# Halved feed-forward steps moved side by side into a block's first half, with their VectorE chains alternating

## The chip, the cores and the metric

The kernel runs on one NeuronCore of one Trainium2 chip. The metric is the device time of one execution in microseconds (us). The kernel before takes 614.94 us, the median of 3 runs (614.88 to 615.11). Engine names are those of the profile: PE is TensorE, DVE VectorE, ACT ScalarE, POOL GpSimd, SP SyncE. An engine's queue runs strictly in the order in which the kernel's Python emits its instructions.

## The reference

`x` is 8 x 3008 x 256 in f32. The first stage is the real part of a two-dimensional Fourier transform over the sequence (3008) and the features (256); the second is a feed-forward layer over the 24,064 tokens:

```python
X = np.fft.fft(np.fft.fft(x, axis=1), axis=2).real      # 8 x 3008 x 256
h = np.maximum(X.reshape(24064, 256) @ w_in, 0.0)       # w_in 256 x 2048
out = (h * h) @ w_out                                   # w_out 2048 x 256
```

## The kernel before

**What is computed.** The transform over the features is multiplied into `w_in` (the three tables `gh`), so that the kernel has only the transform over the sequence left, in f16: `zc` (cosine half) and `zs` (sine half), 128 feature rows by token columns. Symmetry makes one column serve two tokens, k and S-k: with p = gh0·zc and q = gh1·zs, the two tokens' hidden values are p + q and p - q, apart from a term for the row d = 128, which sits in row 0 of `zs`.

**Blocks and steps.** The 12,040 columns are cut into 25 windows (240, 512, 376, 376, 512, 448, eighteen of 512, 360), one block each, numbered from 0. A block has 8 steps; a step makes 256 of the 2048 hidden rows, for both tokens of the window's columns. During block w the second feed-forward product of block w-1 runs as well (`ffn2_steps`, L618, 16 matmuls of 256 columns a step), and so does the Fourier product of the image half whose columns begin in block w+1 (`z_steps`, L480: 12 matmuls of 376 columns for a half called e = 0, 20 shorter ones for e = 1; none in some blocks). Each Fourier half gives `zc` and `zs`: a first sum goes to `es` (ACT, L485); after the second sum ACT writes the near columns (L489) and DVE the far ones ("minus", L496).

**A plain step** (`pq`, `turn`, `square`): four matmuls of p + q (L730, L731), ACT takes max(.,0) into a buffer `h1` (L740), DVE squares `h1` into `h2` (L745) or, for the steps in `by_act`, ACT does (L743); two more matmuls turn the sum into p - q (L736), and ACT and DVE do the same again. `h1` has three buffers, the hidden values' PSUM tile `ph` two.

**A halved step** (`half_q`, `half_p`) saves two matmuls: q alone (L755), ACT writes -2q to `sn` (L758), p is added (L764), ACT copies p + q to `hd` (L767), and DVE makes the rest: two rows `eb`·`wv` for the d = 128 term (L769), their sum with `sn` (L770), the second token's values (L771), max (L773) and square (L774) of both. The first three are called the row sum here, the last three the halves. `sn` has two buffers, `hd` four.

**The d = 128 row** (`row_spread`): ACT's queue sends row 0 of the next block's `zs` to DRAM (`zr`, L579), and SP's queue reads it back into all 128 partitions (`eb`, L581). SP's queue also issues all stores of the output (L598), behind the output's PSUM evacuations by ACT (L633).

**What sets the order.** The order is written out by hand. `PLAN` gives the halved steps and the `by_act` steps of each block by a load number: `load` counts 2 if the block has the second part of an image's folding (`fold_at`), 1 if it has the first (`first_at`), 1 if it has the late folds (`late_at`). Loads of 0 and 1: blocks 3, 6, 7, 11, 14, 17 and 20 to 24, four halved steps; higher loads: 5, 8, 9, 10, 12, 13, 15, 16, 18 and 19, three; blocks 0, 1, 2 and 4 have none. The list `at[s]` holds the folding that step s emits: `d_even`, `n_cos`, `d_odd`, `n_sin`, `odds`, `even` (DVE; `d_odd` also starts the next image's load and `even` the store `scr` on POOL's queue), `back` (four reads `rb` on POOL's queue) and the late folds. `nyq` sends a few values over PE into `py` (PSUM) and back by DVE (L377). In steps 0 to 6 `others(s)` emits, in this order, `at[s]`, the 16 second-product matmuls with their evacuation, `post[s]`, and a share of the Fourier matmuls; in a plain step it stands between `square(s, 0)` and `turn(s)`, in a halved step between `half_q` and `half_p`.

Of the kernel before, what the change touches and what calls it, by code (L numbers as in the profile page):

```python
# [8 lines left out]
F32 = mybir.dt.float32  # L9
# [3 lines left out]
ALU = mybir.AluOpType  # L13

HS = 32.0
P = 128
# [3 lines left out]
def rev_dim(ap, i):  # L20

    dims = [list(d) for d in ap.ap]
    step, cnt = dims[i]
    dims[i] = [-step, cnt]
    return bass.AP(tensor=ap.tensor, offset=ap.offset + step * (cnt - 1), ap=dims)
# [3 lines left out]
def kernel(  # L29
# [14 lines left out]
    nc = tc.nc  # L44
# [12 lines left out]
    FIRST = [240, 512, 376, 376, 512, 448]  # L57
    R23 = float(2.0 ** 23)

    PLAN = {4: ((1, 2, 4, 5), (0, 3, 6)), 3: ((1, 3, 5), (2, 4, 6)), 2: ((1, 4), (0, 3, 6)), 0: ((), ())}  # L60

    RQ = (1, 3, 5, 0, 2, 4)

# [17 lines left out]
    NW = len(wins)  # L81
# [31 lines left out]
    ps_o = ctx.enter_context(tc.tile_pool(name="ps_o", bufs=2, space=bass.MemoryType.PSUM))  # L113
# [170 lines left out]
    at = const.tile([P, 2, P + 1], F32, name="at")  # L284
# [51 lines left out]
    def fold_steps(i):  # L336
# [34 lines left out]

        def nyq():

            py = ps_o.tile([P, 512], F32, name="py", tag="po")
            nc.tensor.matmul(py[:, 0:1], perm[0], od[:, 0, 0, 128:129], start=True, stop=True)
            nc.tensor.matmul(py[:, 1:6], perm[1], rev_dim(od[:, 0, 1:6, 128:129], 1).rearrange("p r o -> p (r o)"), start=True, stop=True)
            nc.vector.tensor_copy(od[:, 1, :, 0:1], py[:, 0:6].rearrange("p (r o) -> p r o", o=1))  # L377
# [148 lines left out]
    def run(*jobs):  # L526
        for j in jobs:
            j()
# [137 lines left out]
    def plan(w):  # L666

        if w < 3 or w == 4:
            return PLAN[0]
        load = 2 * (w in fold_at) + (w in first_at) + (w in late_at)  # L670
        return PLAN[(4, 4, 3)[min(load, 2)]]

    def halved(w):

        return plan(w)[0]
# [4 lines left out]
    for w in range(NW):  # L680
        g0, wn = wins[w]
        h2 = h2p.tile([P, NFC, 2 * WN], F16, name="h2", tag="h2")
        zcw, zsw = zwin(w)

        lo, hi = 0, NST - 1
        at = [[] for _ in range(NST)]
        post = [[] for _ in range(NST)]
        if w == 0:
            at[2] = [f0s["even"], f0s["back"]]
        elif w == 1:  # L690
            fj = fold_jobs(1)
            at = [[f] for f in fj[0:5]] + [[], [], []]
            post[5] = fj[5:6]
            lo, hi = 6, 7
        elif w == 2:
            te = table_steps(1)
            at = [[folds[1]["even"], lambda: te["freq"](), lambda: te["args"](0)], [lambda: te["turns"](0)], [lambda: te["mods"](0)],
                  [lambda: te["absm"](0)], [lambda: te["sins"](0)], [lambda: te["coss"](0)], [], [lambda: te["weigh"]()]]
            for st in range(4):
                at[st + 3] = at[st + 3] + f0s["late"][st : st + 1]  # L700
            at[7].append(folds[1]["back"])
        elif w in fold_at:
            fj = jobs_of.pop(fold_at[w])
            at = [fj[2:3], [], fj[3:4], fj[4:5], [], fj[6:7], fj[7:8], []]
            post[7] = fj[5:6]
        elif w == win_of(col_of[1, 1]) - 1:
            for st in range(4):
                at[st] = folds[1]["late"][st : st + 1]
            lo = 4
        if w in late_at:  # L710
            for st in range(4):
                at[st + 3] = at[st + 3] + folds[late_at[w]]["late"][st : st + 1]
        if w in first_at:
            fj = jobs_of[first_at[w]] = fold_jobs(first_at[w])
            at[0] = at[0] + fj[0:1]
            at[2] = at[2] + fj[1:2]
        if w == 2:
            at[2].append(row_weights)
        zj, zl = [], []
        for u in need[w + 1]:  # L720
            zu = z_steps(u)
            zj += [(zu, 0, 0), (zu, 1, 0), (zu, 0, 1), (zu, 1, 1)]
        f2 = ffn2_steps(*old) if old else []
        phs = {}

        def pq(s):
            ph = phs[s] = ps_h.tile([P, 2, 512], F32, name="ph", tag="psh")
            for a in range(2):
                f0 = (2 * s + a) * P
                nc.tensor.matmul(ph[:, a, 0:wn], gh[:, 0, f0 : f0 + P], zcw[:, 0:wn], start=True, stop=False)  # L730
                nc.tensor.matmul(ph[:, a, 0:wn], gh[:, 1, f0 : f0 + P], zsw[:, 0:wn], start=False, stop=True)  # L731

        def turn(s):
            for a in range(2):
                f0 = (2 * s + a) * P
                nc.tensor.matmul(phs[s][:, a, 0:wn], gh[:, 2, f0 : f0 + P], zsw[:, 0:wn], start=False, stop=True, skip_group_check=True)  # L736

        def square(s, sg):
            h1 = h1p.tile([P, 2, 512], F16, name="h1", tag="h1")
            nc.scalar.activation(h1[:, :, 0:wn], phs[s][:, :, 0:wn], AF.Relu)  # L740
            hv = rev_dim(h1[:, :, 0:wn], 2) if sg else h1[:, :, 0:wn]
            if sg == 0 and s in by_act:
                nc.scalar.activation(h2[:, 2 * s : 2 * s + 2, 0:wn], hv, AF.Square)  # L743
            else:
                nc.vector.tensor_tensor(h2[:, 2 * s : 2 * s + 2, sg * wn : (sg + 1) * wn], hv, hv, op=ALU.mult)  # L745

        two = halved(w)
        by_act = plan(w)[1]
        sns, hds = {}, {}

        def half_q(s):
            ph = phs[s] = ps_h.tile([P, 2, 512], F32, name="ph", tag="psh")
            for a in range(2):
                f0 = (2 * s + a) * P
                nc.tensor.matmul(ph[:, a, 0:wn], gh[:, 1, f0 : f0 + P], zsw[:, 0:wn], start=True, stop=True)  # L755
            i = ROT[0] % 2
            sn = sns[s] = const.tile([P, 2, 2, WN], F16, name=f"sn{i}", tag=f"w16_{i}")
            nc.scalar.activation(sn[:, 0, :, 0:wn], ph[:, :, 0:wn], AF.Copy, bias=0.0, scale=-2.0)  # L758

        def half_p(s):  # L760
            ph, sn = phs[s], sns[s]
            for a in range(2):
                f0 = (2 * s + a) * P
                nc.tensor.matmul(ph[:, a, 0:wn], gh[:, 0, f0 : f0 + P], zcw[:, 0:wn], start=False, stop=True, skip_group_check=True)  # L764
            hd = tmp.tile([P, 2, 2 * WN], F16, name="hd", tag=("tt", "tm")[ROT[0] % 2])
            ROT[0] += 1
            nc.scalar.activation(hd[:, :, 0:wn], ph[:, :, 0:wn], AF.Copy, bias=0.0, scale=1.0)  # L767
            for a in range(2):
                nc.vector.tensor_scalar(out=sn[:, 1, a, 0:wn], in0=eb[w][:, 0:wn], scalar1=wv[:, 2 * s + a : 2 * s + a + 1], scalar2=None, op0=ALU.mult)  # L769
            nc.vector.tensor_tensor(sn[:, 0, :, 0:wn], sn[:, 0, :, 0:wn], sn[:, 1, :, 0:wn], op=ALU.add)  # L770
            nc.vector.tensor_tensor(rev_dim(hd[:, :, wn : 2 * wn], 2), hd[:, :, 0:wn], sn[:, 0, :, 0:wn], op=ALU.add)  # L771
            hv = hd[:, :, 0 : 2 * wn]
            nc.vector.tensor_scalar(out=hv, in0=hv, scalar1=0.0, scalar2=None, op0=ALU.max)  # L773
            nc.vector.tensor_tensor(h2[:, 2 * s : 2 * s + 2, 0 : 2 * wn], hv, hv, op=ALU.mult)  # L774

        def others(s):
            for j in at[s]:
                j()
            for j in spread(f2, s, NST):
                j()  # L780
            for j in post[s]:
                j()
            if s == lo:
                zl[:] = [j for zu, part, h in zj for j in zu(part, h)]
            if s >= lo:
                for j in spread(zl, s - lo, hi - lo) if s < hi else []:
                    j()


        ng = 2 if w == 0 or wins[w - 1][1] < 384 < wn else 1  # L790
        for s0 in range(0, NST, ng):
            ss = range(s0, s0 + ng)
            if s0 in two:
                half_q(s0)
                others(s0)
                half_p(s0)
                continue
            for s in ss:
                pq(s)
            for s in ss:  # L800
                square(s, 0)
            if s0 == hi and w + 1 < NW and halved(w + 1):
                row_spread(w + 1)
            others(s0)
            for s in ss:
                turn(s)
            for s in ss:
                square(s, 1)
            for s in ss[1:]:
                others(s)  # L810
            if s0 < hi <= s0 + ng - 1 and w + 1 < NW and halved(w + 1):
                row_spread(w + 1)
        old = (w, h2)
# [32 lines left out]
```

## Time and profile before

| | |
|---|---|
| median of 3 runs | 614.94 us (614.88 to 615.11) |
| the profiled execution | 615.19 us, of which the span of its instructions is 612.8 us |
| PE, ACT, DVE busy | 96%, 84%, 81% of the span |
| granted PE clock | 0.999 |
| first matmul of block 7, 12, 13, 17, 18, 19, 20 | 162.70, 285.54, 308.60, 405.39, 430.17, 455.78, 480.25 us |
| last block (24) begins | 577.45 us |

A block's first matmul is its first L730 row in the trace, and a block's length is the distance to the next block's. Sums below are made against the profiled execution (612.8 us of span and 2.4 us around it); it is 0.25 us above the median of the runs.

### The profile page before, as it was taken

The numbers are of one execution on the slowest core, as the hardware profiler recorded it, in microseconds if no ns is written. First come the engines' busy times: TensorE is split into PE (matmuls) and PEld (weight loads), VectorE is DVE, ScalarE is ACT, GpSimd is POOL, SyncE is SP. The second block draws the span as 40 slices with busy tenths as digits, with TensorE's granted clock in tenths as the row PEclk, the third lists the DMA queues.
The fourth block names the chain that finished last, engine by engine and source line by source line (L and its number), as shares of the span: only waits on it lengthen the run. The fifth ranks groups of instructions, "written<-read, shape, count | busy, mean of one in ns | idle before, by whom it ended". The sixth has DMA issues, their size and how long they took to land.

```text
span 612.8 us, 11635 instructions
## 1 busy us (share of the span) xinstructions
PE 589.3 (96%) x4416; PEld 424.8 (69%) x4416; DVE 495.4 (81%) x838; ACT 517.3 (84%) x673; POOL 82.5 (13%) x125
## 2 busy tenths in 40 slices
PE   5799999999999999999999999999899999999997
PEld 2456776776677777777777777776577667677786
DVE  7887679696999898968987898858987697887880
ACT  7687788898898898998989889898789888898872
POOL 5343100012002202020023001220010200000000
PEclk9999999999999999999999999999999999999999
DMA  8927221183114623631155121551112311211112
GB/s 146 217 68 148 61 73 35 42 177 81 52 42 90 167 59 68 151 91 55 51 112 136 58 61 48 105 146 55 48 33 64 122 35 48 57 46 44 60 56 66
DMA packets 39592, 50.21 MB, mean 82 GB/s; under 512 B 4572, under 2 KB 33393, under 8 KB 39537
## 3 DMA queue, kind: packets, MB, share of 16 engines
q0 software_dynamic: 9344, 22.14, 18.0%
q1 hardware_dynamic: 29923, 27.11, 15.1%
q8 instruction: 34, 0.56, 0.4%
q10 hardware_dynamic: 270, 0.23, 0.1%
q14 instruction: 21, 0.17, 0.1%
HBM read 36.29 MB, written 27.86 MB: 105 GB/s over the span
## 4 chain that ended last, share of the span: by engine, by line
PE 61%; DVE 16%; ACT 10%; issue 5%; DMA 4%; SPq 2%; POOL 1%; DVEq 0%; ACTq 0%; POOLq 0%
PE po L618 36%; PE ph L736 5%; PE ph L730 5%; PE ph L731 5%; ACT h L740 4%; PE ph L764 3%; PE ph L755 3%; DVE h L774 3%; DMA eb<-zr 3%; DVE hd L773 2%; DVE hd L771 2%; SPq L598 2%; PE pz L480 2%; DVE h L745 2%; ACT sn L758 2%
## 5 line engine op out<-in xcount | busy, mean ns | idle before, releaser
L618 PE MATMUL po<-wout,h 128*128 128x256 f16 (+1 forms) x3024 | 362.2, 273 | 3.2 <-DVE od L377 1.1
L618 PEld LDWEIGHTS <-h 128*128 128x128 f16 (+1 forms) x3024 | 296.4, 98 | 75.3 <-DVE h L745 1.8
L740 ACT ACTIVATE h<-ph 128x1024 f16<-128x1024 f32 (+4 forms) x252 | 235.6, 962 | 28.6 <-PE ph L736 15.5
L745 DVE TENSOR_TENSOR h<-h 128x1024 f16<-128x1024 f16 (+4 forms) x189 | 118.1, 641 | 56.1 <-ACT h L740 47.9
L731 PE MATMUL ph<-zs,gh 128*128 128x512 f16 (+4 forms) x252 | 90.9, 363 | 1.2 <-DVE zs L496 0.9
L730 PE MATMUL ph<-zc,gh 128*128 128x512 f16 (+4 forms) x252 | 91.0, 363 | 1.1 <-ACT h L740 0.8
L774 DVE TENSOR_TENSOR h<-hd 128x2048 f16<-128x2048 f16 (+3 forms) x74 | 87.9, 1188 | 2.5
L767 ACT ACTIVATE hd<-ph 128x1024 f16<-128x1024 f32 (+3 forms) x74 | 73.6, 994 | 15.0 <-PE ph L764 14.6
L633 ACT ACTIVATE osb<-po 128x512 f32<-128x512 f32 (+3 forms) x95 | 54.9, 581 | 28.4 <-PE po L618 21.5
L758 ACT ACTIVATE sn<-ph 128x1024 f16<-128x1024 f32 (+3 forms) x74 | 73.4, 992 | 0.0
L736 PE MATMUL ph<-zs,gh 128*128 128x512 f16 (+4 forms) x252 | 69.9, 363 | 2.1 <-ACT h L740 1.0
L743 ACT ACTIVATE h<-h 128x1024 f16<-128x1024 f16 (+3 forms) x63 | 64.8, 1029 | 2.0
L771 DVE TENSOR_TENSOR hd<-hd,sn 128x1024 f16<-128x1024 f16 (+3 forms) x74 | 49.8, 673 | 19.4 <-ACT hd L767 13.4
L770 DVE TENSOR_TENSOR sn<-sn 128x1024 f16<-128x1024 f16 (+3 forms) x74 | 49.8, 673 | 7.4 <-ACT hd L767 0.5
L773 DVE TENSOR_SCALAR hd<-hd 128x2048 f16<-128x2048 f16 (+3 forms) x74 | 49.9, 675 | 2.5
L769 DVE TENSOR_SCALAR sn<-eb,wv 128x512 f16<-128x512 f16 (+3 forms) x148 | 44.6, 343 | 8.2 <-DMA eb<-zr 8.2
L764 PE MATMUL ph<-zc,gh 128*128 128x512 f16 (+3 forms) x148 | 42.8, 370 | 2.6 <-ACT sn L758 1.8
L731 PEld LDWEIGHTS <-gh 128*128 128x128 f16 x252 | 24.6, 98 | 27.4 <-issue 2.5
L730 PEld LDWEIGHTS <-gh 128*128 128x128 f16 x252 | 24.5, 97 | 26.5 <-issue 1.7
L755 PE MATMUL ph<-zs,gh 128*128 128x512 f16 (+3 forms) x148 | 42.9, 371 | 0.0
L423 POOL COPY xt<-xt 128x2 f16<-128x2 f16 x16 | 5.6, 379 | 215.4 <-DVE xt L406 215.4
L736 PEld LDWEIGHTS <-gh 128*128 128x128 f16 x252 | 23.2, 97 | 9.6 <-issue 4.3
(121 smaller groups left out, 377.7 us busy)
## 6 DMA issues: line engine op xcount, KB each, us to landing
out_dram<-osb SPq DMA_DIRECT2D x77, 128.0 KB
xo<-in_x_dram POOLq DMA_DIRECT2D x7, 768.0 KB
scr<-ev POOLq DMA_DIRECT2D x8, 390.0 KB, 3.9
eb<-zr SPq DMA_DIRECT2D x18, 128.0 KB
rb<-scr POOLq DMA_DIRECT2D x16, 130.0 KB
out_dram<-osb SPq DMA_DIRECT2D x12, 94.0 KB
w<-in_moe_w_in_dram POOLq DMA_DIRECT2D x2, 512.0 KB
wout<-in_moe_w_out_dram POOLq DMA_DIRECT2D x1, 1024.0 KB
```

The lines of the kernel that those rows point to most:

```text
L618: nc.tensor.matmul(po[0:m, j * D : (j + 1) * D], h2[:, fc, q : q + m], wout16[:, fc, :], start=(fc == 0), stop=(fc == NFC - 1))
L730: nc.tensor.matmul(ph[:, a, 0:wn], gh[:, 0, f0 : f0 + P], zcw[:, 0:wn], start=True, stop=False)
L731: nc.tensor.matmul(ph[:, a, 0:wn], gh[:, 1, f0 : f0 + P], zsw[:, 0:wn], start=False, stop=True)
L736: nc.tensor.matmul(phs[s][:, a, 0:wn], gh[:, 2, f0 : f0 + P], zsw[:, 0:wn], start=False, stop=True, skip_group_check=True)
L740: nc.scalar.activation(h1[:, :, 0:wn], phs[s][:, :, 0:wn], AF.Relu)
L743: nc.scalar.activation(h2[:, 2 * s : 2 * s + 2, 0:wn], hv, AF.Square)
L745: nc.vector.tensor_tensor(h2[:, 2 * s : 2 * s + 2, sg * wn : (sg + 1) * wn], hv, hv, op=ALU.mult)
L758: nc.scalar.activation(sn[:, 0, :, 0:wn], ph[:, :, 0:wn], AF.Copy, bias=0.0, scale=-2.0)
L767: nc.scalar.activation(hd[:, :, 0:wn], ph[:, :, 0:wn], AF.Copy, bias=0.0, scale=1.0)
L771: nc.vector.tensor_tensor(rev_dim(hd[:, :, wn : 2 * wn], 2), hd[:, :, 0:wn], sn[:, 0, :, 0:wn], op=ALU.add)
L773: nc.vector.tensor_scalar(out=hv, in0=hv, scalar1=0.0, scalar2=None, op0=ALU.max)
L774: nc.vector.tensor_tensor(h2[:, 2 * s : 2 * s + 2, 0 : 2 * wn], hv, hv, op=ALU.mult)
```

## The change

1. The halved steps stand side by side in a block's first half, and the `by_act` steps change: `PLAN` now has ((1, 2, 3, 4), (0, 6)) for load 0, ((1, 2, 3, 4), (0, 5, 6)) for load 1 and ((1, 2, 3), (0, 5, 6)) above. The number of halved steps of every block stays as it was.
2. A halved step's DVE work is cut in two. The row sum is emitted right behind `half_q`, ahead of `others(s)`; the halves are emitted one step later, alternating with the next step's row sum instruction by instruction, or, where the next step is plain, around its first square.
3. Of the Fourier product's second sums the sine comes first, and `row_spread` is emitted in step 6, behind `square(6, 0)` (before: in step 7, behind `square(7, 0)`).
4. `n_cos` moves from step 2 to step 5, `n_sin` from 2 to 4, `odds` from 3 to 5, `even` from 5 to 6, `back` from 6 to 7.
5. `py` takes a bank of the Fourier product's PSUM pool instead of one of the second product's (images from 2 on).

```diff
-    PLAN = {4: ((1, 2, 4, 5), (0, 3, 6)), 3: ((1, 3, 5), (2, 4, 6)), 2: ((1, 4), (0, 3, 6)), 0: ((), ())}
+    PLAN = {0: ((1, 2, 3, 4), (0, 6)), 1: ((1, 2, 3, 4), (0, 5, 6)), 2: ((1, 2, 3), (0, 5, 6))}
...
-            py = ps_o.tile([P, 512], F32, name="py", tag="po")
+            py = (ps_z if i > 1 else ps_o).tile([P, 512], F32, name="py", tag="pz" if i > 1 else "po")
...
-        load = 2 * (w in fold_at) + (w in first_at) + (w in late_at)
-        return PLAN[(4, 4, 3)[min(load, 2)]]
+        return PLAN[min(2, 2 * (w in fold_at) + (w in first_at) + (w in late_at))]
...
-            at = [fj[2:3], [], fj[3:4], fj[4:5], [], fj[6:7], fj[7:8], []]
+            at = [fj[2:3], [], [], [], fj[3:4], fj[4:5], fj[6:7], fj[7:8]]
...
-            at[2] = at[2] + fj[1:2]
+            at[5] = at[5] + fj[1:2]
...
-            zj += [(zu, 0, 0), (zu, 1, 0), (zu, 0, 1), (zu, 1, 1)]
+            zj += [(zu, 0, 0), (zu, 1, 0), (zu, 1, 1), (zu, 0, 1)]
...
+        def row_sum(s):
...
+            return [
+                lambda: row(0),
+                lambda: row(1),
+                lambda: nc.vector.tensor_tensor(sn[:, 0, :, 0:wn], sn[:, 0, :, 0:wn], sn[:, 1, :, 0:wn], op=ALU.add),
+            ]
+
+        def halves(s):
...
+            return [
+                lambda: nc.vector.tensor_tensor(rev_dim(hd[:, :, wn : 2 * wn], 2), hd[:, :, 0:wn], sn[:, 0, :, 0:wn], op=ALU.add),
+                lambda: nc.vector.tensor_scalar(out=hv, in0=hv, scalar1=0.0, scalar2=None, op0=ALU.max),
+                lambda: nc.vector.tensor_tensor(h2[:, 2 * s : 2 * s + 2, 0 : 2 * wn], hv, hv, op=ALU.mult),
+            ]
...
+            left = halves(s0 - 1) if s0 - 1 in two else []
             if s0 in two:
                 half_q(s0)
+                for j in [j for p in zip(left or [run] * 3, row_sum(s0)) for j in p]:
+                    j()
                 others(s0)
                 half_p(s0)
                 continue
             for s in ss:
                 pq(s)
             for s in ss:
-                square(s, 0)
-            if s0 == hi and w + 1 < NW and halved(w + 1):
+                run(*(left[0:2] + square(s, 0) + left[2:3]))
+            if s0 == hi - 1 and ng == 1 and w + 1 < NW and halved(w + 1):
                 row_spread(w + 1)
```

More of the change, by code (lines that the diff above doesn't have):

```diff
@@ L668, in plan @@
         if w < 3 or w == 4:
-            return PLAN[0]
-        load = 2 * (w in fold_at) + (w in first_at) + (w in late_at)
-        return PLAN[(4, 4, 3)[min(load, 2)]]
+            return (), ()
+        return PLAN[min(2, 2 * (w in fold_at) + (w in first_at) + (w in late_at))]
     def halved(w):
@@ L743, in square @@
                 nc.scalar.activation(h2[:, 2 * s : 2 * s + 2, 0:wn], hv, AF.Square)
-            else:
-                nc.vector.tensor_tensor(h2[:, 2 * s : 2 * s + 2, sg * wn : (sg + 1) * wn], hv, hv, op=ALU.mult)
+                return []
+            return [lambda: nc.vector.tensor_tensor(h2[:, 2 * s : 2 * s + 2, sg * wn : (sg + 1) * wn], hv, hv, op=ALU.mult)]
         two = halved(w)
@@ L767, in half_p, with row @@
             nc.scalar.activation(hd[:, :, 0:wn], ph[:, :, 0:wn], AF.Copy, bias=0.0, scale=1.0)
-            for a in range(2):
+            hds[s] = hd
+        def row_sum(s):
+            sn = sns[s]
+            def row(a):
                 nc.vector.tensor_scalar(out=sn[:, 1, a, 0:wn], in0=eb[w][:, 0:wn], scalar1=wv[:, 2 * s + a : 2 * s + a + 1], scalar2=None, op0=ALU.mult)
-            nc.vector.tensor_tensor(sn[:, 0, :, 0:wn], sn[:, 0, :, 0:wn], sn[:, 1, :, 0:wn], op=ALU.add)
-            nc.vector.tensor_tensor(rev_dim(hd[:, :, wn : 2 * wn], 2), hd[:, :, 0:wn], sn[:, 0, :, 0:wn], op=ALU.add)
-            hv = hd[:, :, 0 : 2 * wn]
-            nc.vector.tensor_scalar(out=hv, in0=hv, scalar1=0.0, scalar2=None, op0=ALU.max)
-            nc.vector.tensor_tensor(h2[:, 2 * s : 2 * s + 2, 0 : 2 * wn], hv, hv, op=ALU.mult)
+            return [
[4 more added lines that the diff above has]
+        def halves(s):
+            sn, hd = sns[s], hds[s]
+            hv = hd[:, :, 0 : 2 * wn]
+            return [
[3 more added lines that the diff above has]
+            ]
         def others(s):
@@ L807 @@
             for s in ss:
-                square(s, 1)
+                run(*square(s, 1))
             for s in ss[1:]:
```

## The prediction

> **What bounds the kernel now.** I read the page's busy shares, busy times by block, the timeline where a block is long, then the waits and the chain of waits.
>
> ```profile
> PE 589.3 (96%) x4416; PEld 424.8 (69%) x4416; DVE 495.4 (81%) x838; ACT 517.3 (84%) x673; POOL 82.5 (13%) x125
> ```
>
> PE is the bound. Columns below: block, length, busy PE, PEld, DVE, ACT, POOL, clock, DMA.
>
> ```profile
> 285.54:308.60 23.06, 23.06 (x171) 16.62 (x170) 21.54 (x35) 20.52 (x24) 1.88 (x4) 1.00 0.18 53
> 405.39:430.17 24.78, 24.67 (x181) 17.60 (x180) 15.54 (x28) 21.98 (x30) 3.08 (x4) 1.00 0.26 80
> 430.17:455.78 25.61, 23.57 (x171) 16.45 (x170) 24.57 (x41) 20.64 (x24) 1.53 (x4) 1.00 0.16 41
> 480.25:506.33 26.08, 24.84 (x181) 17.59 (x180) 20.66 (x37) 22.09 (x30) 2.97 (x4) 1.00 0.22 67
> ```
>
> Block 12 (first row: three halved steps, no Fourier product) has no gap: 23.06 is its floor. Block 18 has the same matmuls and takes 25.61.
>
> ```profile
> 285.54 0.38 PE L730 MATMUL ph<-zc,gh 128*128 128x512 f16 x1
> ...
> 288.58 0.59 PE L755 MATMUL ph<-zs,gh 128*128 128x512 f16 x2
> ...
> 291.20 0.38 PE L730 MATMUL ph<-zc,gh 128*128 128x512 f16 x1
> ...
> 163.96 0.38 PE L731 MATMUL ph<-zs,gh 128*128 128x512 f16 x1 [0.88 <-DVE zs L496]
> ...
> 433.10 0.61 PE L618 MATMUL po<-wout,h 128*128 128x256 f16 x4 [0.81 <-DVE h L774]
> 434.82 0.39 PE L618 MATMUL po<-wout,h 128*128 128x256 f16 x2 [1.11 <-DVE h L745]
> ...
> 482.42 0.81 PE L618 MATMUL po<-wout,h 128*128 128x256 f16 x6 [1.14 <-DVE od L377]
> ```
>
> A plain step is 3.04 (288.58 - 285.54), a halved one 2.62; four halved give 22.64. A Fourier half e = 0 adds 12 x 0.157 = 1.88 (block 9: 24.94 = 23.06 + 1.88), e = 1 1.21. Lengths less floors: block 7 1.67; 8 0.06; 10, 13, 16, 19 0.20 each; 11, 14, 17 0.26 each; 18 2.55; 20 1.56; 21 0.41; 22 0.88; 23 0.70; 9, 12, 15 nothing: 9.4. Gaps between matmul starts add 2.4 in blocks 3 to 6: **11.8 us** is all that better order can win. The rows name DVE as late, in 18 and 20 because `eb` came late a block before:
>
> ```profile
> DVE sn L769 <- DMA eb<-zr: 8.2, 4, 4.9
> ```
>
> ```profile
> 453.29 4.71 SPq L598
> ...
> 458.11 5.42 DMA eb<-zr
> ...
> 463.55 0.63 DVE sn L769 x2
> ```
>
> SP was still issuing a store (4.71) when `eb`'s turn came. The small 0.20 to 0.27 are L764 waiting for `sn`, where a plain step with ACT's square precedes.
>
> **The change, part by part.** *Matmuls*: the same number; floors stay. *Squares*: eight leave ACT (63 to 55, 1.03 each) for DVE (0.60 each); neither is the bound in those blocks.
>
> *Alternation.* The dependent chain and, in the last two rows, neighbours that do not depend on each other:
>
> ```profile
> 302.87 0.61 DVE L769 TENSOR_SCALAR sn<-eb,wv 128x512 f16<-128x512 f16 x2
> 303.58 0.69 DVE L770 TENSOR_TENSOR sn<-sn 128x1024 f16<-128x1024 f16 x1
> 304.38 0.69 DVE L771 TENSOR_TENSOR hd<-hd,sn 128x1024 f16<-128x1024 f16 x1
> 305.10 0.69 DVE L773 TENSOR_SCALAR hd<-hd 128x2048 f16<-128x2048 f16 x1
> 305.83 1.23 DVE L774 TENSOR_TENSOR h<-hd 128x2048 f16<-128x2048 f16 x1
> 306.97 0.42 DVE L417 TENSOR_TENSOR yt<-xt 128x520 f16<-128x520 f16 x1
> 307.31 1.28 DVE L745 TENSOR_TENSOR h<-h 128x1024 f16<-128x1024 f16 x2
> ```
>
> A halved step takes 306.97 - 302.87 = 4.10 now. The L745 pair (1.28 for two of 0.69) starts 0.59 apart, a dependent 0.69 starts 0.72 to 0.80 apart. Alternated: add 0.60, row 0.26, max 0.60, row 0.26, square 1.14, sum 0.79 (the next add needs it) = 3.65. That is 0.45 off DVE's queue for each of 74 steps, 33 us, none of it on PE's path by itself.
>
> *Side by side.* ACT first; its spacings in block 11's rows are L740, L758 and L767 0.92, L740 to its own square 1.05, the square to the next 0.96, L633 0.50, L485 0.36, L489 0.42 for two pieces. In the halved run it has `hd`, `sn` (0.92 each), `osb` 0.50 and `es` 0.36 against 2.62 or more of PE, and no square ahead: the L764 waits of 0.2 to 0.3 go (about 2 us in all). But steps 5 and 6 now both have ACT's square. Take blocks 10, 13, 16 and 19, from step 5's first matmul: L740 starts at 1.12 (behind step 4's second one), the square at 2.17, `osb` at 3.13, `zs` at 3.62, the second L740 at 4.04. PE begins step 6 at 3.23, so that is 0.81 into it; L740 follows at 1.73, the square at 2.78, `zc` at 3.81, and step 6's second L740 0.97 into step 7; step 7's first ends at 2.94, where L736 was due at 0.86 + 1.75 = 2.61. So 0.33 is lost in each; in block 9, whose e = 0 half makes the steps longer, 0.15; without a Fourier half nothing.
>
> DVE: the halves of step 1 can start 1.30 after step 2's first matmul (block 21: 511.99, L771 at 513.30). From there 3.65 a step; DVE falls about 1 us a halved step behind PE and catches up in the plain ones. Who waits for that? `sn` of step s overwrites that of s - 2: free 1 to 2 us before ACT needs it. `h1`: in block 13, with step 1 at 0, the halves start at 4.1, the last row sum ends at 11.4, then add 0.72, max 0.60, step 4's first square 0.60, the halves' square 1.14, `n_sin` 0.87 and the second square of step 4 (0.69) end at 16.02; ACT wants that buffer for step 6 at 16.49. **The margin is 0.47.** The built program gives step 6 another buffer in blocks 8, 9, 12, 15 and 18. In block 7 the third sum ends at 15.05, the halves 0.72 + 0.72 + 1.14 later, `n_cos` 0.87, L496 0.5, the square 0.69: 19.70. ACT wants that buffer in step 7 at 19.42, so L736 is 0.68 late. Where four halved steps stand and step 5's square is ACT's or the buffer is another (6, 11, 14, 17, 20, 21, 23), nothing waits: block 21's 0.41 and block 23's share go.
>
> *py*: block 20's 1.14 wait for L377 goes; the Fourier bank it takes is free about 1 us before.
>
> *Row earlier.* `zr` left 1.97 before a block's end; behind step 6's square it leaves some 3 before. On ACT it now stands ahead of L489, of step 6's second L740 and thus of L736 in step 7. In blocks 6 and 22 it waits for DVE's L496: in 22 at 15.05 + 0.72 + 0.60 + 0.60 + 1.14 + 0.50 = 18.6, then `zc` 0.45 and two L740 end at 21.05, L736 due at 20.1: 0.95 lost; in 6, with two late folds, L496 ends at 19.45 and L736 loses 1.05. The same wait held ACT in block 6 before (block 7's 0.88 row) and made `eb` late for block 23, which now gets it 2 us sooner.
>
> SP's order is unchanged except once, for block 3: `eb` still stands behind step 5's stores. So the late `eb` of block 19, 4.5 after step 1 (463.5 - 459.0), stays: halves 1.9 late, less the margin: 1.45. That of block 17 (landed 415.48, 6.9 after step 1) costs 2.7 if unchanged (`sn` of steps 3 and 4 held 1.9 and 0.8), nothing if 3 us earlier; `even`'s 390 KB and `back`'s four reads (POOL's queue, order unchanged) now come a step after those stores, so I take 2.0.
>
> *Folding later.* DVE work of 0.9 each, already in the times above. `back`'s reads land some 6 us before block 9 needs them (issued about 217, L406 due near 226): nothing.
>
> **Sum.** Left after: blocks 3 and 4 0.6 of 1.5 (block 3 has one ACT square less, about 0.8 at 376 columns; 0 to 1.5 is possible), 6 1.05, 7 0.68, 9 0.15, 10, 13, 16 0.99, 17 2.0, 19 1.45, 22 0.95: 7.9. Gain 11.8 - 7.9 = 3.9. The profiled execution: 615.19 - 3.9 = 611.3; the median, 0.25 lower, 611.0.
>
> **Rivals.** *Slower: alternation saves nothing.* If each instruction waits out its predecessor whether it depends on it or not, a step stays at 4.10, DVE is 0.9 (three halved) or 1.35 (four) later, beyond the margin. Then blocks 6, 7, 22 lose 1.35 each, 10, 13, 16 0.57, 19 0.9, 17 0.8, 23 1.2, 21 0.5, 12, 15, 18 0.3: 10 more, 17.9 left against 11.8: 621. It decides from 0.47 us of lateness per block. For it: DVE has 24.57 busy in block 18. Against: the 0.59 spacing. With any other cause of a backlog beyond the margin it has 0.22.
>
> The Trainium skill, page "VectorE: DVE Perf Modes", section "The DRAIN you can't avoid", says that the next operation does not start until the pipeline has emptied, and that eight chained copies took the same time with and without semaphores between them; by that rule alternation gains nothing and this rival's time holds. The L745 pair, 0.59 apart where a dependent one is 0.72 apart, does not agree with it.
>
> *Given back:* block 17 and 19 as late as before and 0.1 to 0.2 more of ACT's lateness in twenty blocks: 3 us, 614. Chance 0.15.
>
> *Both `eb` in time and no row wait:* 2.7 to 4 left, 606. SP's 4.71 speaks against. Chance 0.13.
>
> **Numbers.** The forecast (608.5 to 613) has 0.50. A measurement can tell about 0.2%, 1.2 us, from no change. Faster: 0.50 + 0.13, less 0.01 at the edge, 0.62; same 0.15; slower 0.23. The range 605 to 618 takes in both middle rivals and the lower part of the slower one.
>
> **What would show it.** Right: L787 to L788 some 0.86 apart with a row between; blocks 18 and 20 at 23.1 and 24.5; no L764 wait above 0.1 in blocks 11 and 14; block 19 long by over 1. Wrong: L739 waiting for DVE L744 in most blocks (first rival), or `eb` landing early in 17 and 19.

## The result and the profile after

The change makes the kernel slower: 618.62 us (median of 4 runs, 618.38 to 620.64) against 614.91 us for the kernel before on the same chip, a ratio of 1.0069 with a 95% interval of 1.0047 to 1.0091. The prediction said 611.0 and a range of 605 to 618. The profiled execution took 620.64 us (span 618.7); its start-up ahead of block 2 is 2.2 us longer than before. From block 2 on, the lengths of the blocks add up to 558.32 us, before to 554.63: **3.69 us longer**, close to the distance of the medians (3.71). Lengths in this text are differences of first matmuls (for block 24, up to the end of the last matmul), so that the start-up doesn't enter.

The lines of the changed kernel, where they differ from those named above: L729 and L730 are p + q (a block's first matmul is an L729 row here), L735 the turn to p - q, L739 ACT's max, L742 and L744 the squares of ACT and DVE, L754 and L757 q and `sn`, L763 and L766 p and `hd`, L774 and L779 the row sum, L787 to L789 the halves.

First the page's busy times:

```profile
PE 590.1 (95%) x4416; PEld 426.1 (69%) x4416; DVE 486.8 (79%) x846; ACT 510.5 (83%) x665; POOL 76.0 (12%) x125
```

DVE and ACT have less work than before and PE has as many matmuls. So no other engine became the bound: PE waits more. Busy times by block (block bounds, length, busy PE, PEld, DVE, ACT, POOL, granted clock, DMA share, GB/s), for blocks 12, 17, 18, 20 and 10:

```profile
292.04:315.16 23.12, 23.12 (x172) 16.62 (x171) 20.03 (x33) 20.37 (x24) 1.15 (x4) 1.00 0.16 48
414.50:439.02 24.52, 24.52 (x182) 17.62 (x181) 19.34 (x36) 20.90 (x29) 3.08 (x4) 1.00 0.28 78
439.02:462.13 23.11, 23.11 (x171) 16.61 (x170) 20.35 (x34) 20.36 (x24) 1.14 (x4) 1.00 0.16 46
488.28:512.80 24.52, 24.52 (x182) 17.61 (x180) 19.60 (x36) 20.90 (x29) 3.50 (x4) 1.00 0.28 79
241.67:267.53 25.86, 24.77 (x194) 18.07 (x192) 20.83 (x32) 22.39 (x30) 3.28 (x4) 1.00 0.52 117
```

Blocks 18 and 20 fell from 25.61 and 26.08 to 23.11 and 24.52, as forecast. But block 10, 24.47 before, takes 25.86, and PE is idle for 1.09 of it. The waits (engine, tile, line, what it waited for: us in total, times, longest) name, in the first row here, a pair that the view of before does not have at all:

```profile
PE pz L480 <- ACT es L485: 7.6, 9, 1.0
...
DVE sn L774 <- DMA eb<-zr: 4.7, 3, 2.2
```

The timeline of block 10, step 3, all engines (start, duration, engine, line, out<-in, idle time before it and its releaser):

```profile
251.66 1.02 ACT L757 ACTIVATE sn<-ph 128x1024 f16<-128x1024 f32 x1
...
252.72 0.25 PE L480 MATMUL pz<-cos,spn 128*128 128x94 f16 x2
...
252.92 0.60 ACT L633 ACTIVATE osb<-po 128x512 f32<-128x512 f32 x1 [0.24 <-PE po L618]
253.41 0.48 ACT L485 ACTIVATE es<-pz 128x377 f32<-128x377 f32 x1
...
253.94 0.24 PE L480 MATMUL pz<-sin,xt 128*128 128x188 f16 x1 [0.98 <-ACT es L485]
```

**This is where the time went.** A Fourier half keeps two PSUM tiles `pz`, one for `zc` and one for `zs`, and the second sum is added onto the first in the same tile, after ACT has copied the first sum to `es`. Before, the sums came in the order cosine first, sine first, cosine second, sine second: a whole other sum lay between a copy and the matmuls that write over its source. Edit 3 puts the second sine sum right behind the first sine sum. In an e = 1 half the border between the two falls inside a step, in block 10 inside step 3: the last two matmuls of the first sum (252.72) and the first of the second (253.94) stand next to each other in PE's queue, and the second has to wait for L485. That is no bare 0.48 us of copying: L485 stands behind L633 in ACT's queue and ends at 253.89. The distance between the starts of these matmuls exceeds their own time by 1.13 us in blocks 7, 10, 13, 16, 19 and 22, and by 0.73 in blocks 3 and 4: **8.3 us** (the view of waits counts PE's idle time alone, 0.98 of the 1.13). The ninth wait of the view, 0.57 us in an e = 0 half, lies in block 1; in the e = 0 halves from block 2 on there is no such gap.

The second largest new gap is block 6's end:

```profile
164.22 0.60 DVE L496 SCALAR_TENSOR_TENSOR zs<-es,pz 128x102 f16<-128x102 f32 x2
164.51 0.22 ACTq L579 DMA_DIRECT2D zr<-zs  x1
...
164.90 0.60 ACT L633 ACTIVATE osb<-po 128x512 f32<-128x512 f32 x1 [1.78 <-DMA zr<-zs]
...
167.76 0.59 PE L735 MATMUL ph<-zs,gh 128*128 128x512 f16 x2 [1.73 <-ACT h L739]
```

ACT's last instruction had ended at 163.13; its queue stood at L579, which had to wait for DVE's L496, and PE lost 1.89 us a step later.

### The profile page after: what moved, and what is told of

It reads as the page before. It is cut to its first block, busy times and chain, and to the rows that moved or that the text cites. A ratio compares the mean times of both kernels' runs of the same rounds, so it can differ in the third digit from the quotient of the medians.

```text
span 618.7 us, 11663 instructions
## 1 busy us (share of the span) xinstructions
PE 590.1 (95%) x4416; PEld 426.1 (69%) x4416; DVE 486.8 (79%) x846; ACT 510.5 (83%) x665; POOL 76.0 (12%) x125
## 4 chain that ended last, share of the span: by engine, by line
PE 72%; DVE 10%; ACT 8%; issue 4%; DMA 4%; POOL 1%; SPq 0%; ACTq 0%; DVEq 0%; POOLq 0%
PE po L618 42%; PE ph L735 6%; PE ph L729 6%; PE ph L730 6%; PE ph L763 4%; PE ph L754 4%; ACT h L739 4%; PE pz L480 3%; DVE h L744 2%; DMA w<-in_moe_w_in_dram 1%; DMA eb<-zr 1%; DVE hd L787 1%; DVE hd L788 1%; DVE h L789 1%; ACT osb L633 1%
## 5 line engine op out<-in xcount | busy, mean ns | idle before, releaser
L618 PE MATMUL po<-wout,h 128*128 128x256 f16 (+1 forms) x3024 | 361.6, 273 | 0.0
L618 PEld LDWEIGHTS <-h 128*128 128x128 f16 (+1 forms) x3024 | 296.6, 98 | 71.3
L739 ACT ACTIVATE h<-ph 128x1024 f16<-128x1024 f32 (+4 forms) x252 | 231.5, 962 | 28.1 <-PE ph L735 18.0
L744 DVE TENSOR_TENSOR h<-h 128x1024 f16<-128x1024 f16 (+4 forms) x197 | 125.1, 643 | 78.4 <-ACT h L739 71.2
L766 ACT ACTIVATE hd<-ph 128x1024 f16<-128x1024 f32 (+3 forms) x74 | 73.5, 994 | 27.1 <-PE ph L763 27.0
L729 PE MATMUL ph<-zc,gh 128*128 128x512 f16 (+4 forms) x252 | 91.0, 363 | 1.1 <-ACT h L739 0.8
L730 PE MATMUL ph<-zs,gh 128*128 128x512 f16 (+4 forms) x252 | 90.9, 363 | 0.4 <-ACT zs L489 0.4
L789 DVE TENSOR_TENSOR h<-hd 128x2048 f16<-128x2048 f16 (+3 forms) x74 | 87.3, 1179 | 0.1
L633 ACT ACTIVATE osb<-po 128x512 f32<-128x512 f32 (+3 forms) x95 | 54.8, 580 | 26.9 <-PE po L618 22.5
L735 PE MATMUL ph<-zs,gh 128*128 128x512 f16 (+4 forms) x252 | 70.0, 363 | 4.7 <-ACT h L739 3.2
L757 ACT ACTIVATE sn<-ph 128x1024 f16<-128x1024 f32 (+3 forms) x74 | 73.7, 995 | 0.0
L787 DVE TENSOR_TENSOR hd<-hd,sn 128x1024 f16<-128x1024 f16 (+3 forms) x74 | 49.7, 672 | 20.7 <-ACT hd L766 15.4
L742 ACT ACTIVATE h<-h 128x1024 f16<-128x1024 f16 (+3 forms) x55 | 56.9, 1034 | 1.7
L774 DVE TENSOR_SCALAR sn<-eb,wv 128x512 f16<-128x512 f16 (+3 forms) x148 | 48.9, 342 | 4.7 <-DMA eb<-zr 4.7
L779 DVE TENSOR_TENSOR sn<-sn 128x1024 f16<-128x1024 f16 (+3 forms) x74 | 49.3, 666 | 2.2
L788 DVE TENSOR_SCALAR hd<-hd 128x2048 f16<-128x2048 f16 (+3 forms) x74 | 49.5, 669 | 0.7
L763 PE MATMUL ph<-zc,gh 128*128 128x512 f16 (+3 forms) x148 | 42.8, 370 | 0.8 <-ACT sn L757 0.8
L730 PEld LDWEIGHTS <-gh 128*128 128x128 f16 x252 | 24.6, 98 | 27.4 <-issue 2.5
L754 PE MATMUL ph<-zs,gh 128*128 128x512 f16 (+3 forms) x148 | 42.9, 371 | 0.0
L729 PEld LDWEIGHTS <-gh 128*128 128x128 f16 x252 | 24.5, 97 | 25.5 <-issue 0.5
L735 PEld LDWEIGHTS <-gh 128*128 128x128 f16 x252 | 23.8, 97 | 12.9 <-issue 7.6
```

The costliest lines, as they stand in the source:

```text
L618: nc.tensor.matmul(po[0:m, j * D : (j + 1) * D], h2[:, fc, q : q + m], wout16[:, fc, :], start=(fc == 0), stop=(fc == NFC - 1))
L633: nc.scalar.activation(osb[0:mm].rearrange("p s d -> p (s d)")[:, lo:hi], po[0:mm, lo:hi], AF.Copy, bias=0.0, scale=HS * HS)
L744: return [lambda: nc.vector.tensor_tensor(h2[:, 2 * s : 2 * s + 2, sg * wn : (sg + 1) * wn], hv, hv, op=ALU.mult)]
L789: lambda: nc.vector.tensor_tensor(h2[:, 2 * s : 2 * s + 2, 0 : 2 * wn], hv, hv, op=ALU.mult),
```

## The experiments

The kernels ran beside the kernel before, whose medians in these sessions were 614.6 to 615.9 us; ratios are against those. The theories: **E**, the second sine sum waits for `es`; **R**, the row sent in step 6 holds ACT's queue; **S**, the halved steps side by side overload DVE or ACT. Besides the medians each experiment is read by its blocks (us; "2 to 24" is the sum of these lengths):

| kernel | median | 2 to 24 | 3 + 4 | 6 | 7 | 10 | 11 | 18 | 19 | 20 | 22 |
|---|---|---|---|---|---|---|---|---|---|---|---|
| before | 614.91 | 554.63 | 41.53 | 23.66 | 25.52 | 24.47 | 24.78 | 25.61 | 24.47 | 26.08 | 24.73 |
| after | 618.62 | 558.32 | 43.03 | 25.47 | 25.36 | 25.86 | 24.52 | 23.11 | 26.15 | 24.52 | 25.02 |
| sine_apart | 610.79 | 550.19 | 41.51 | 25.47 | 24.23 | 24.61 | 24.52 | 23.11 | 24.74 | 24.52 | 24.50 |
| edit3_undone | 607.48 | 546.91 | 41.59 | 23.57 | 23.99 | 24.37 | 24.52 | 23.11 | 24.73 | 24.52 | 23.99 |
| edit3_alone | 620.13 | 558.80 | 42.97 | 24.93 | 25.39 | 25.40 | 24.78 | 24.04 | 25.40 | 24.78 | 25.76 |
| edit2_alone | 610.80 | 550.98 | 41.53 | 23.66 | 24.32 | 24.47 | 24.78 | 24.22 | 24.47 | 25.74 | 24.29 |
| row_in_7 | 608.34 | 547.45 | 41.51 | 23.57 | 24.23 | 24.61 | 24.52 | 23.11 | 24.72 | 24.52 | 23.88 |
| row_back | 617.61 | 556.44 | 43.02 | 23.58 | 25.37 | 25.86 | 24.52 | 23.11 | 26.15 | 24.52 | 25.03 |
| serial_chain | 622.32 | 562.34 | 42.15 | 23.57 | 24.99 | 24.86 | 25.61 | 23.51 | 26.18 | 25.61 | 25.36 |
| py_in_po | 607.58 | 548.33 | 41.59 | 23.57 | 23.99 | 24.37 | 24.52 | 23.11 | 24.72 | 24.74 | 23.99 |
| plan_before | 609.90 | 548.85 | 41.53 | 23.66 | 24.31 | 24.47 | 24.78 | 23.07 | 24.47 | 24.78 | 24.29 |

**sine_apart**: the wait for `es` taken away by the order alone.

```diff
-            zj += [(zu, 0, 0), (zu, 1, 0), (zu, 1, 1), (zu, 0, 1)]
+            zj += [(zu, 1, 0), (zu, 0, 0), (zu, 1, 1), (zu, 0, 1)]
```

> The changed kernel with one line different: the Fourier sums go sine first, cosine first, sine second, cosine second, so that the sine half still ends first but a cosine sum stands between its two sums. Theory E (the change loses because the second sine sum follows the first in the same PSUM bank within one step, and TensorE waits for ScalarE's copy to es: L480 rows of 1.13 us in six blocks and 0.73 in two, 8.3 us): 618.6 - 8.3 = 610.3 us, no L480 gap above 0.2. Theory S (the loss comes from the halved steps standing side by side: VectorE's backlog or ScalarE's two squares): the order of the sums does not touch it, 617 to 619. Theory R (the row, sent in step 6, holds ScalarE for VectorE): also unchanged, 617 to 619.

Measured: 610.79 us, ratio to before 0.9934 (0.9912 to 0.9956). The same place of block 10 in its timeline, the rows of L480 and of ACT:

```profile
248.06 0.25 PE L480 MATMUL pz<-cos,yt 128*128 128x94 f16 x2
...
248.15 0.24 PE L480 MATMUL pz<-sin,xt 128*128 128x188 f16 x1
...
248.26 0.60 ACT L633 ACTIVATE osb<-po 128x512 f32<-128x512 f32 x1 [0.24 <-PE po L618]
...
248.75 0.48 ACT L485 ACTIVATE es<-pz 128x377 f32<-128x377 f32 x1
```

The second sine sum starts 0.09 us behind the matmul before it, ahead of a copy that is still pending: that copy is now the cosine's. ACT's queue is as it was. By the blocks 558.32 - 550.19 = 8.13 us are gone, and no L480 gap is left. E holds, to half a microsecond of its number; the change without this wait is faster than before. Block 6 stays at 25.47.

**edit3_undone**: the changed kernel with the sums in their old order and the row back in step 7.

```diff
-            zj += [(zu, 0, 0), (zu, 1, 0), (zu, 1, 1), (zu, 0, 1)]
+            zj += [(zu, 0, 0), (zu, 1, 0), (zu, 0, 1), (zu, 1, 1)]
...
-            if s0 == hi - 1 and ng == 1 and w + 1 < NW and halved(w + 1):
+            if s0 == hi and w + 1 < NW and halved(w + 1):
```

> The changed kernel with edit 3 taken back whole: sums in the order of before, the row sent in step 7 again; halved steps side by side, alternation, later folding and py's bank stay. E: the 8.3 us go, and with them whatever the earlier row cost (1.9 us in block 6) or won: 608 to 610.5. S: 617 to 619. R: about 616.5, the L480 gaps being cover for something else.

Measured: 607.48 us, ratio 0.9888 (0.9864 to 0.9912). That is slightly below E's 608. Edits 1, 2, 4 and 5 save 7.72 us by the blocks; edit 3 costs 11.41 on top. S falls. By the blocks this is the fastest order of the sums and place of the row that was run.

**edit3_alone**: before with these two hunks of edit 3 and nothing else.

> The kernel before with edit 3 alone: sine second sum right behind its first, row in step 6. E: the same wait appears in the eight blocks with an e = 1 half, 1.1 to 1.4 us each where a plain step with ScalarE's square precedes: 615 + 8 to 11 = 623 to 626. S: edit 3 costs nothing by itself, 614 to 616. R: 616 to 618, the row waiting for VectorE in blocks 6, 9 and 22.

Measured: 620.13 us, ratio 1.0091 (1.007 to 1.0112). The gaps are there without the rest of the change (1.13 us in blocks 10, 13, 16 and 19, 1.44 in 7 and 22, 0.73 in 3 and 4: 8.9 in all), so they don't need the new DVE order. The kernel lost less than I expected, since blocks 18 and 20 fell to 24.04 and 24.78. Block 17 first uses its `eb` at 8.52 in the block, where it was 10.09 before. The earlier row need not be the reason: in sine_apart and row_in_7, which differ by the row's step alone, it is 7.33 and 7.31. That a PE that waits lets the late `eb` and DVE catch up fits this, but was not tested by itself.

**edit2_alone**: before with the halved step's DVE work cut in two, deferred and alternated.

> The kernel before with edit 2 alone: row sum ahead of the step's other work, halves one step later, alternating; halved steps where they were. E: no loss from it; VectorE's queue is 0.4 us shorter a halved step, so the waits of blocks 18 and 20 shrink: 611 to 614. S, if the deferral is what hurts: above 616. A theory that alternation saves nothing: 614 to 616.

Measured: 610.80 us, ratio 0.9936 (0.9915 to 0.9956), slightly below what was expected: 3.65 us by the blocks, in 7, 18, 20, 22 and 23. This is the edit as a whole; it does not tell the earlier row sum, the deferral and the alternation apart.

**row_in_7** and **row_back**: the row's place by itself. Each puts the row back into step 7 (second hunk of edit3_undone), the first in sine_apart, the second in the changed kernel.

> The changed kernel with the two sine sums first and third (sine_apart) and the row sent in step 7 as before, so that from sine_apart only the row's place differs, and from edit3_undone only the order of the sums. Theory R: the 3.3 us that sine_apart is longer than edit3_undone are the row's, which in step 6 holds ScalarE's queue until VectorE has written zs: about 607.5, block 6 back from 25.47 to 23.6, block 22 from 24.50 to 24.0, no L735 waits of 0.2 to 0.4 behind L376 in blocks 10, 13 and 16. Rival O: the order of the sums moves the same 3.3 us (zs ready at another time): 610.8, block 6 stays at 25.47.

> The changed kernel with the row sent in step 7 as before and the order of the sums as changed, which completes the square of order and row: changed order with row in 6 (618.6), apart with row in 6 (610.8), apart with row in 7 (608.3). Theory E: the two costs are separate, so 2.7 us go with the row (block 6 from 25.47 to about 23.7) and the wait for es stays in blocks 3, 4, 7, 10, 13, 16, 19, 22 (about 1.1 each, 0.7 in the first two): about 616, still slower than before. Rival: the wait for es makes room for the row in part, so that less than 1 us goes: 618. Rival W: the early row alone made the change slow, and with the row back it is faster than before: below 612.

Measured: row_in_7 608.34 us, ratio 0.9874 (0.9822 to 0.9926); row_back 617.61 us, ratio 1.0035 (1.0013 to 1.0058). With the sums apart the row costs 550.19 - 547.45 = 2.74 us (1.90 in block 6, 0.62 in block 22, 0.17 in 16). With the sums as changed it costs 558.32 - 556.44 = 1.88 and block 6 alone: block 22's part is covered by the wait for `es`. Rival O has a small share: 547.45 - 546.91 = 0.54: 0.24 each in blocks 7, 10, 13 and 16 stays when the row goes back, and blocks 17 and 22 give back 0.33. I expected about 616 for row_back; the median of its ten runs (616.35 to 619.79) came out higher; the blocks of the profiled one say 1.9 us. Block 6's rows of row_back show what the step did:

```profile
162.30 0.22 ACTq L579 DMA_DIRECT2D zr<-zs  x1
...
162.56 1.04 ACT L739 ACTIVATE h<-ph 128x1024 f16<-128x1024 f32 x1
...
163.65 0.59 PE L735 MATMUL ph<-zs,gh 128*128 128x512 f16 x2
```

L739 follows 0.26 behind L579 and PE's L735 has no wait. The wait for `es` is unchanged in row_back's waits, to the digit:

```profile
PE pz L480 <- ACT es L485: 7.6, 9, 1.0
```

**serial_chain**: edit3_undone, alternation taken back, deferral kept.

```diff
-                for j in [j for p in zip(left or [run] * 3, row_sum(s0)) for j in p]:
+                for j in left + row_sum(s0):
...
-                run(*(left[0:2] + square(s, 0) + left[2:3]))
+                run(*(left + square(s, 0)))
```

> edit3_undone with its two VectorE chains one behind the other, not alternated: the halves of the step before are issued whole, then the row and its sum; in plain steps the halves whole, then the square. The instructions and their step stay the same. Theory A: the alternation is worth 0.45 us of VectorE's time per halved step (4.10 for 3.65), and the backlog then goes past the margin: add 0.57 in blocks 10, 13, 16, 0.9 in 19, 0.8 in 17, 1.2 in 23, 0.5 in 21, 0.3 in 12, 15, 18: 6.0 more, about 613.5. Rival H: the halved steps are slower on VectorE, but the deferral leaves so much room that nobody waits: 607.5 to 608.5. Rival D: an instruction waits out its predecessor whether it depends on it or not, so the pitch of a halved step is the same in both, and so is the time, 607.5.

Measured: 622.32 us, ratio 1.0101 (1.0056 to 1.0146): 15.4 us more than edit3_undone by the blocks. DVE's rows alone, first of serial_chain (block 12), then of the changed kernel (block 10):

```profile
294.49 0.69 DVE L787 TENSOR_TENSOR hd<-hd,sn 128x1024 f16<-128x1024 f16 x1 [0.65 <-ACT hd L766]
295.22 0.69 DVE L788 TENSOR_SCALAR hd<-hd 128x2048 f16<-128x2048 f16 x1
295.94 1.23 DVE L789 TENSOR_TENSOR h<-hd 128x2048 f16<-128x2048 f16 x1
297.09 0.61 DVE L774 TENSOR_SCALAR sn<-eb,wv 128x512 f16<-128x512 f16 x2
297.80 0.69 DVE L779 TENSOR_TENSOR sn<-sn 128x1024 f16<-128x1024 f16 x1
298.60 0.69 DVE L787 TENSOR_TENSOR hd<-hd,sn 128x1024 f16<-128x1024 f16 x1
```

```profile
252.83 0.69 DVE L787 TENSOR_TENSOR hd<-hd,sn 128x1024 f16<-128x1024 f16 x1
253.44 0.35 DVE L774 TENSOR_SCALAR sn<-eb,wv 128x512 f16<-128x512 f16 x1
253.71 0.68 DVE L788 TENSOR_SCALAR hd<-hd 128x2048 f16<-128x2048 f16 x1
254.31 0.34 DVE L774 TENSOR_SCALAR sn<-eb,wv 128x512 f16<-128x512 f16 x1
254.57 1.22 DVE L789 TENSOR_TENSOR h<-hd 128x2048 f16<-128x2048 f16 x1
255.71 0.68 DVE L779 TENSOR_TENSOR sn<-sn 128x1024 f16<-128x1024 f16 x1
256.49 0.69 DVE L787 TENSOR_TENSOR hd<-hd,sn 128x1024 f16<-128x1024 f16 x1
```

The same six instructions take 298.60 - 294.49 = 4.11 us one behind the other and 256.49 - 252.83 = 3.66 alternated. Rival D falls on its first claim, the pitch, and A's pitch holds. The 15.4 us are not the pitch's alone, though. The second hunk also moves something: in the plain step behind the halved ones, DVE's first square (L744) now stands behind the halves' square (L789) instead of ahead of it. Where that square is ACT's, the hunk changes nothing; of these blocks, 6 and 21 lose 0.00, and block 7 loses 1.00, of which PE waits 0.82 at its start for DVE's L496 of block 6. Blocks 11, 14 and 20 lose 1.10 each. The rows of block 11, first of serial_chain, then of edit3_undone:

```profile
282.46 0.69 DVE L788 TENSOR_SCALAR hd<-hd 128x2048 f16<-128x2048 f16 x1
283.19 1.23 DVE L789 TENSOR_TENSOR h<-hd 128x2048 f16<-128x2048 f16 x1
284.33 0.68 DVE L744 TENSOR_TENSOR h<-h 128x1024 f16<-128x1024 f16 x1
285.11 1.02 ACT L739 ACTIVATE h<-ph 128x1024 f16<-128x1024 f32 x1 [1.24 <-DVE h L744]
```

```profile
278.42 0.69 DVE L788 TENSOR_SCALAR hd<-hd 128x2048 f16<-128x2048 f16 x1
279.03 0.68 DVE L744 TENSOR_TENSOR h<-h 128x1024 f16<-128x1024 f16 x1
279.63 1.22 DVE L789 TENSOR_TENSOR h<-hd 128x2048 f16<-128x2048 f16 x1
281.06 1.03 ACT L739 ACTIVATE h<-ph 128x1024 f16<-128x1024 f32 x1
```

Counted from the block's first matmul (261.92 and 259.22), L744 starts 22.41 - 19.81 = 2.60 later. The L788 ahead of it starts 1.34 later, which is the chains' pitch; the other 1.26 are the square's new place. With the pitch alone L744 would end at 21.83 by this estimate, and ACT wanted the buffer at 21.84, so that block would have lost next to nothing. How much of the 15.4 the alternation of the chains is worth stays open, and with it A's price of 6 and rival H; no run took back the first hunk alone. The waits of serial_chain show who pays, ACT for a free `h1` and then PE for ACT:

```profile
ACT h L739 <- DVE h L744: 16.1, 18, 2.1
...
PE ph L735 <- ACT h L739: 11.9, 18, 1.8
```

In edit3_undone these are 1.0, 3 and 1.2, 5.

**py_in_po**: edit3_undone with `py` in the bank of `po` (the line of before).

> edit3_undone with py in the bank of po, as before edit 5. Theory P: block 20's wait of L618 for L377 comes back, 1.14 us, and nothing else: about 608.6. Rival N: with the halves spread differently VectorE reaches L377 in time, 607.5.

Measured: 607.58 us, ratio 0.9851 (0.981 to 0.9893); no difference to edit3_undone that the medians show. Block 20, where L618 waited 1.14 for L377 before, is 0.22 longer with the old bank. Block 17 is 1.20 longer in the profiled execution, where DVE's first L774, which waits for `eb`, starts 7.0 us after SP issued it (405.56 to 412.55) instead of 5.7. I cannot tell from one profile whether that has to do with the edit; the other kernels have anything from 3.5 to 7.1 us there. N is nearer than P.

**plan_before**: edit3_undone with the old `PLAN` and `plan`, so edits 2, 4 and 5.

> edit3_undone with the PLAN and the plan function of before, so that edits 2, 4 and 5 are in and edits 1 and 3 are not. Theory S: the halved steps side by side take away the L763 waits in blocks 11, 14, 17, 20 (0.26 each), 21 and 23 (0.31 each), and part of 18: 1.5 to 2 us: about 609.3. Rival T: the plan is all that lies between edit2_alone and edit3_undone (edits 4 and 5 are worth nothing): 610.8. Rival U: the plan is worth nothing once the chains are alternated: 607.5.

Measured: 609.90 us, ratio 0.99 (0.9854 to 0.9945). S, by the blocks: 548.85 - 546.91 = 1.94, mostly 0.26 each in blocks 11, 14 and 20 and 0.31 each in 7, 21, 22 and 23. Against edit2_alone, edits 4 and 5 bring 550.98 - 548.85 = 2.13, in blocks 18 (1.15) and 20 (0.96).

Together, in us over blocks 2 to 24, each on top of those named before it (the parts are not independent: with the sums apart the row costs 2.74): edit 2 -3.65, edits 4 and 5 -2.13, edit 1 -1.94, the sums in another order 0.54, the second sine sum behind the first 8.99 (row_back less row_in_7), the row in step 6 1.88: 3.69.

## Why the prediction was wrong

**The step that failed is "Matmuls: the same number; floors stay", with "Row earlier".** I priced edit 3 as what it does to the row: ACT's queue, SP's order, L496. That from block 2 on it also moves eight groups of matmuls onto the heels of a copy that reads the same PSUM tile was not asked. The trace of before could not show the wait, as there it never came up, but the code says that the second sum is added in place, and the price was in the rows I used: in the halved steps ACT has `sn`, `osb` (0.50) and `es` (0.36 by spacing, 0.48 to its end) to do behind each other while PE's next matmul is due at once. None of my rivals had it, and none of the signs that I had listed bears on it: those of a right forecast (the spacing of L787 and L788, blocks 18 and 20, the L764 waits in 11 and 14, a long block 19) all appeared in a kernel that became slower. The 621 of the first rival is near the result, but its mechanism is not what happened: the pitch is 3.66.

**The other terms.** Left after the change I had 7.9 us; the measured 15.5 (11.8 and the 3.69) are 8.3 of waits for `es` and 7.2 of the rest. That the rest comes so near is partly luck, as its terms show:

- *Alternation*: 3.65 forecast, 3.66 measured. The first rival's condition is false. Its price is not settled: serial_chain loses 15.4, where I had 10 with the row's blocks and 6 without, but it moves the plain step's square as well, and block 21, for which I had 0.5, lost nothing.
- *Side by side*: blocks 10, 13 and 16 lose 0.33 in steps 6 and 7 by the forecast, and 0.09 + 0.23 = 0.32 in the trace. The two squares alone don't do it: edit3_undone has them too and loses nothing there (block 10 at 24.37). It takes ACT's `zs` copies between them, which the forecast had counted and only the new order of the sums puts there. The L764 waits (now L763) in 11 and 14 are gone; block 9 loses nothing where I had 0.15.
- *Blocks 18, 20*: 23.11 and 24.52 (23.1 and 24.5). For block 20 I gave the reason to edit 5. py_in_po shows 0.22 for it once the other edits are in.
- *Row earlier*, block 6: 1.05 forecast, 1.89 measured, and of the 0.90 that stood there before 0.82 stayed too. The wait chain was right; L496 came later than counted (first one done at 21.75 in the block, for 19.45). Block 22: 0.95 forecast; 0.62 in sine_apart, none beside the `es` wait.
- *Late eb*: both terms too large. For block 17 I had 2.7 if `eb` came as late as before, nothing if 3 us earlier, and took 2.0. Its first use came at 6.35 in the block, 3.74 earlier than before (10.09) though 1.28 behind block 14's place (5.07), and nothing was lost. In py_in_po, where it came at 8.73, block 17 lost 1.43, in two waits for `sn` as forecast: the path was right and the arrival was not. Block 19 (1.45) lost 0.61 in steps 6 and 7, only 0.29 more than block 10. Its DVE work was late by 1.74, close to the 1.9 forecast. The wait for `es` is not what hid the rest: in edit3_undone, which has no such wait, the DVE work is 1.73 late and block 19 loses 0.36 more than block 10. The margin of 0.47, taken over from block 13, was too small for it.
- *Blocks 3 and 4*: forecast to gain 0.9; without the `es` wait they are unchanged (41.51 and 41.53).

**The first rival's rule.** The Trainium skill, page "VectorE: DVE Perf Modes", section "The DRAIN you can't avoid", does say that the next operation does not start until the pipeline has emptied, but the same paragraph adds that a next operation that is not held starts earlier. The prediction left that out, so it does not follow from the section that alternation gains nothing. The runs show independent neighbours starting earlier: an instruction of 0.68 to 0.69 us is followed after 0.60 to 0.61 by one that doesn't need it (252.83, 253.44; 253.71, 254.31) and after 0.72 to 0.80 by one that does (294.49, 295.22; 297.80, 298.60).

## What to carry to other kernels

When an edit changes the order of matmuls, list for each PSUM tile who reads it between two groups that write it. An accumulation that goes on in place after a copy has the copy as a predecessor, with all that stands ahead of the copy in its engine's queue; put another tile's sum between the two, and the wait is gone (sine_apart; its order of the sums costs 0.54 against the old one). Take the parts of a change apart on the chip: here four of five edits were worth 7.7 us and the fifth, which looked like the smallest, cost 11.4. Cutting long dependent VectorE chains in two, deferred and alternated, was worth 3.65 by itself; where a deferred piece stands in the queue matters too, for the next step's square behind it held ACT and then PE.

## What the runs showed of the hardware that was not expected

- A PSUM copy of 0.48 us costs the matmul behind it 1.13 us: it starts 0.49 behind ACT's 0.60 us evacuation (252.92, 253.41), and PE's next matmul starts 0.05 after its end (253.89, 253.94).
- The same DMA (`eb` for block 17, 128 KB written from one row) took from 3.5 us (row_back, 412.41 to 415.92) to 7.1 us (the kernel before, 408.39 to 415.48) from SP's issue to the first use, with DVE waiting for it each time. What sets it was not found.
- Waits don't add up: block 22's row wait of 0.62 vanishes behind the 1.13 in the same block.
